# Issuing the first weight transfer of a decode kernel ahead of the entry barrier of the engines

## The chip, the cores and the metric

The kernel runs on one core of a Trainium2 chip. The third batch of runs was on another chip than the first two, so times are compared within a batch. The metric is the device time of one execution in microseconds (us), smaller is better. One execution in each set is also profiled; its span (first to last instruction of the program) is about 1.8 us shorter than the measured time.

Engines are called TensorE (PE in the profile; PEld is its weight load), VectorE (DVE), ScalarE (ACT), GpSimd (POOL) and SyncE (SP). A `q` behind an engine (SPq) marks work of its sequencer, such as issuing a transfer.

## The reference, cut to what matters

One decode step for four sequences: attention over a cache of 8192 keys, and a gated MLP, mixed by a gate.

```python
# B=4, Sq=1, D=1024, H=32, Sk=8192, Dh=128, F=3584; all bfloat16
q = (x @ wq)                                       # wq 1024 x 4096: 8 MB
scores = einsum("bhqd,bhkd->bhqk", q, k_cache) * Dh ** -0.5     # k_cache 256 MB
o = einsum("bhqk,bhkd->bhqd", softmax(scores), v_cache)         # v_cache 256 MB
a = o.reshape(B, 1, H * Dh) @ wo                   # wo 8 MB
b = x + sigmoid(r) * ((silu(x @ w_gate) * (x @ w_up)) @ w_down) # S=1: every row is chosen
return g * a + (1 - g) * b
```

Each key and value is used for one query only, so nearly all of the work is moving 576 MB (549 MiB) from HBM. Sizes called MB in the rest of this text are units of 2^20 bytes, except in lines and rates of the profile.

## The kernel before

All large inputs go through a ring of five slots of 4 MB in SBUF. SyncE issues every ring transfer, in program order; a transfer is issued when the engine that last read its slot has finished with it. K passes through VectorE, which transposes it into a tile T with two buffers, and TensorE multiplies T; V goes straight to TensorE.

```python
ring = const.tile([P, NS, RING], BF, name="ring")          # NS = 5 slots of 4 MB

def load_pair(src, n, apart=False):
    a = slots(2)
    if a + 1 < NS and not apart:                           # one transfer over two slots
        nc.sync.dma_start(out=flat[:, lo:lo + 2 * n], in_=src)
    ...                                                    # else one transfer for each slot

nc.scalar.dma_start(out=x6[0:Bn], in_=x2)                  # and two more tiny loads into x6
...
def k_pair(d):                                             # cut
    ks = load_pair(kv_view(A_k_cache, d), RING)
    for n in range(RD):                                    # 8 pieces
        T = ttp.tile(..., tag="T")                         # bufs=2
        nc.vector.transpose(out=T[...], in_=kn[...])       # frees the slot after piece 4 and 8
        ... 8 matmuls on T ...

def v_pair(d):                                             # cut: the last pair
    vs = [ring[:, slots(1)] for _ in range(2)]
    nc.sync.dma_start(out=vs[0], in_=vv[:, 0:RING])        # 4 MB in one transfer
    for c in range(4):
        nc.sync.dma_start(out=vs[1][:, lo:hi], in_=vv[:, RING + lo:RING + hi])   # 1 MB each
```

The order is: wq, w_gate, then K pairs, w_up, w_down, K and V pairs in turn, and wo at the end. The program begins with a barrier of all engines, made by the framework: each engine drains, GpSimd collects the arrivals and releases all (in the profile of before the drains begin at 0.00 to 0.37 us, GpSimd's two semaphore records stand at 0.59 and 0.67 us, the releases of the others at 0.71 to 0.72 us).

## Time and profile before

| | |
|---|---|
| time, first three runs | 1347.67 us median (1346.08 to 1349.52) |
| span of the profiled run | 1345.3 us |
| TensorE, VectorE busy | 78%, 46% |
| mean granted TensorE clock | 0.91 |
| first packet of the ring | 1.81 us after the program's first instruction |

The page of the kernel before. The second part gives 40 equal slices of the span, with the busy share of the 16 DMA engines in tenths; the third the share of the 16 engines' time that each queue used:

```profile
span 1345.3 us, 7987 instructions
...
DMA  9999999999999999999999999999999999999997
GB/s 413 427 436 427 442 429 425 443 431 419 443 435 419 437 435 433 433 433 430 435 435 435 435 431 431 427 428 434 435 423 442 433 419 431 431 427 440 426 426 318
...
q1 hardware_dynamic: 13976, 575.68, 99.3%
```

The queue is busy from end to end at about 430 GB/s.

The timeline of the kernel before (start, duration, engine, line, operation; in brackets the idle time of the engine before it and what ended it), at the start:

```profile
0.79 0.56 ACTq L122 DMA_DIRECT2D x<-in_A_x_dram  x1
0.80 0.40 SPq L109 DMA_DIRECT2D ring<-in_A_wq_dram  x1
1.25 0.41 SPq L109 DMA_DIRECT2D ring<-in_B_w_gate_dram  x1
...
15.84 0.62 PE L139 MATMUL small<-identb,x 6*128 6x6 bf16 x8 [15.84 <-DMA x<-in_gate_w_dram]
23.21 6.51 PE L226 MATMUL S_ps<-ring,xw 128*4 128x512 bf16 x64 [0.56 <-DMA ring<-in_A_wq_dram]
...
50.85 2.31 DVE L352 STREAM_TRANSPOSE T<-ring 128x2048 uint32<-128x2048 uint32 x1 [17.02 <-DMA ring<-in_A_k_cache_dram]
```

SyncE stands at the barrier from 0.00 to 0.71 us (the trace's records of its drain and release) and issues wq only then. The last line is the first use of K.

The same timeline around the issue of a later K transfer, and at the end of the program:

```profile
1106.94 4.51 DVE L352 STREAM_TRANSPOSE T<-ring 128x2048 uint32<-128x2048 uint32 x2 [3.13 <-DMA ring<-in_A_k_cache_dram]
1109.40 3.57 PE L358 MATMUL S_ps<-T,Z 128*128 128x512 bf16 x8 [7.10 <-DVE T L352]
...
1117.94 4.51 DVE L352 STREAM_TRANSPOSE T<-ring 128x2048 uint32<-128x2048 uint32 x2 [2.48 <-PE S_ps L358]
1120.28 0.33 SPq L109 DMA_DIRECT2D ring<-in_A_k_cache_dram  x1
...
1316.38 13.11 PE L429 MATMUL o_ps<-ring,PB 128*32 128x512 bf16 x60 [1.86 <-DMA ring<-in_A_v_cache_dram]
1335.32 7.07 PE L192 MATMUL acc<-ring,LT 128*4 128x512 bf16 x32 [0.36 <-DVE LT L291]
```

Here the issue at 1120.28 us waits for VectorE, which had waited 2.48 us for TensorE, which ran its eight matmuls in 3.57 us (granted clock 0.5 from 1107.69 us for 10.24 us) where the same group takes 1.90 us elsewhere (at 923.22 us, granted clock 1.0).

### The profile page before, as it was taken

How to read it: one execution, taken by the hardware profiler on the slowest of the kernel's cores; microseconds unless marked ns; L12 is line 12 of the kernel's file. 1: busy time of each engine (PE TensorE's matmuls, PEld its weight loads, DVE VectorE, ACT ScalarE, POOL GpSimd, SP SyncE). 2: the span in 40 equal slices, each digit the busy share in tenths (PEclk: the TensorE clock that was granted, in tenths of full speed). 3: DMA queues.
4: the chain of work that ended last, by engine and by line, in shares of the span. 5: the costliest groups of instructions: out<-in, count | busy, mean ns of one | idle time of the engine just before them, and what ended most of it. 6: DMA issues, size and time to landing. Idle time of an engine off the chain costs nothing.

```text
span 1345.3 us, 7987 instructions
## 1 busy us (share of the span) xinstructions
PE 1050.1 (78%) x4536; PEld 229.2 (17%) x2348; DVE 623.1 (46%) x358; ACT 51.4 (4%) x46; POOL 59.0 (4%) x91
## 2 busy tenths in 40 slices
PE   2565977777887778878977779697779679877888
PEld 0111111112111111111211111111111112111211
DVE  4465655534445553345455456146555254556000
ACT  0000100001000100001000010001000010000000
POOL 4000100001000100001000010000000010000000
PEclk9787988988998888899898889898899798989999
DMA  9999999999999999999999999999999999999997
GB/s 413 427 436 427 442 429 425 443 431 419 443 435 419 437 435 433 433 433 430 435 435 435 435 431 431 427 428 434 435 423 442 433 419 431 431 427 440 426 426 318
DMA packets 14031, 576.20 MB, mean 428 GB/s; under 512 B 1566, under 2 KB 1574, under 8 KB 2092
## 3 DMA queue, kind: packets, MB, share of 16 engines
q1 hardware_dynamic: 13976, 575.68, 99.3%
q8 instruction: 27, 0.44, 0.1%
q14 instruction: 8, 0.07, 0.0%
q10 hardware_dynamic: 20, 0.02, 0.0%
HBM read 575.68 MB, written 0.01 MB: 428 GB/s over the span
## 4 chain that ended last, share of the span: by engine, by line
DMA 58%; PE 23%; DVE 10%; issue 8%; ACT 0%; DVEq 0%; SPq 0%; POOL 0%
DMA ring<-in_A_k_cache_dram 50%; PE S_ps L358 11%; PE o_ps L429 11%; DVE T L352 10%; DMA ring<-in_A_v_cache_dram 5%; DMA ring<-in_B_w_gate_dram 3%; PE small L448 1%; PE acc L192 1%; PE o_ps L226 0%; ACT OS L441 0%; DVEq L352 0%; DVE OS L442 0%; ACT res L495 0%; SPq L109 0%; POOL Z L335 0%
## 5 line engine op out<-in xcount | busy, mean ns | idle before, releaser
L352 DVE STREAM_TRANSPOSE T<-ring 128x2048 uint32<-128x2048 uint32 x256 | 570.6, 2282 | 501.4 <-DMA ring<-in_A_k_cache_dram 425.9
L358 PE MATMUL S_ps<-T,Z 128*128 128x512 bf16 x2048 | 536.7, 410 | 220.8 <-DVE T L352 214.8
L429 PE MATMUL o_ps<-ring,PB 128*32 128x512 bf16 x2048 | 460.5, 387 | 37.6 <-DMA ring<-in_A_v_cache_dram 37.6
L358 PEld LDWEIGHTS <-Z 128*128 128x128 bf16 x1024 | 106.2, 104 | 643.6 <-issue 635.8
L429 PEld LDWEIGHTS <-PB 128*32 128x32 bf16 x1024 | 100.7, 99 | 395.2 <-issue 373.1
L383 ACT ACTIVATE PTs<-S_ps,negm 128x1024 bf16<-128x1024 f32 x8 | 8.9, 1114 | 994.7 <-DVE negm L380 994.7
L335 POOL TENSOR_TENSOR Z<-qa,mq 128x16 bf16<-128x16 bf16 x32 | 8.3, 262 | 808.4 <-PE S_ps L358 737.3
L442 DVE SCALAR_TENSOR_TENSOR OS<-o_ps,mE,OS 128x512 f32<-128x512 f32 x8 | 6.0, 751 | 68.8 <-ACT OS L441 68.8
L394 POOL COPY PB<-PT 32x1024 bf16<-32x1024 bf16 x16 | 30.4, 1897 | 26.8 <-DVE rex L396 26.5
L392 ACT COPY PB<-PT 32x1024 bf16<-32x1024 bf16 x16 | 30.6, 1914 | 10.7 <-DVE PT L385 10.6
L291 DVE CAST LT<-small 128x64 bf16<-128x64 f32 x2 | 0.4, 224 | 46.3 <-PE small L289 46.3
L376 POOL PARTITION_ALL_REDUCE gmx<-mex x8 | 3.2, 396 | 340.6 <-DVE mex L373 340.6
L371 DVE TENSOR_REDUCE m<-S_ps 128x1 f32<-128x1024 f32 x8 | 9.8, 1225 | 15.9 <-PE S_ps L358 15.9
L402 DVE RECIPROCAL rinv<-tot 128x16 f32<-128x16 f32 x8 | 2.0, 248 | 31.1 <-POOL tot L398 31.1
L385 DVE STREAM_TRANSPOSE PT<-PTs 128x1024 bf16<-128x1024 bf16 x8 | 10.0, 1245 | 12.1 <-ACT PTs L383 12.1
L192 PE MATMUL acc<-ring,LT 128*4 128x512 bf16 x64 | 14.5, 379 | 0.7 <-DVE LT L291 0.7
L139 PE MATMUL small<-identb,x 6*128 6x6 bf16 x8 | 0.6, 196 | 15.8 <-DMA x<-in_gate_w_dram 15.8
L448 PEld LDWEIGHTS small<-selg,OS 128*128 128x128 f32 x64 | 11.8, 260 | 7.0 <-issue 4.9
L192 PE MATMUL acc<-ring,hT 128*4 128x512 bf16 x56 | 12.2, 379 | 0.0
L448 PE MATMUL small<-selg,OS 128*128 128x16 f32 x64 | 10.6, 302 | 0.9 <-DVE OS L442 0.9
L226 PE MATMUL o_ps<-ring,xw 128*4 128x512 bf16 x56 | 4.9, 481 | 7.1 <-DMA ring<-in_B_w_gate_dram 7.1
L441 ACT ACTIVATE OS<-o_ps,mE 128x512 f32<-128x512 f32 x8 | 5.5, 687 | 120.2 <-PE o_ps L429 120.2
(71 smaller groups left out, 82.2 us busy)
## 6 DMA issues: line engine op xcount, KB each, us to landing
ring<-in_A_v_cache_dram SPq DMA_DIRECT2D x15, 4096.0 KB, 30.1
ring<-in_A_k_cache_dram SPq DMA_DIRECT2D x14, 4096.0 KB, 31.8
ring<-in_B_w_gate_dram SPq DMA_DIRECT2D x1, 7168.0 KB
ring<-in_B_w_up_dram SPq DMA_DIRECT2D x1, 7168.0 KB
ring<-in_B_w_down_dram SPq DMA_DIRECT2D x2, 3584.0 KB
ring<-in_A_wo_dram SPq DMA_DIRECT2D x6, 1024.0 KB, 27.0
ring<-in_A_v_cache_dram SPq DMA_DIRECT2D x4, 1024.0 KB, 34.0
ring<-in_A_wo_dram SPq DMA_DIRECT2D x4, 512.0 KB, 17.3
```

Source lines behind the costliest of these rows:

```text
L192: nc.tensor.matmul(out_ap, lhsT=lhsT, rhs=rhs, start=start, stop=True, skip_group_check=True)
L335: nc.gpsimd.tensor_tensor(out=Z[:, :, QP - 1:QP - 1 + P].rearrange("p e (q c) -> p e q c", c=QP)[:, :, :, 0], in0=qa[:, :, h0:h0 + NQ, b], ...
L352: nc.vector.transpose(out=T[:].rearrange("p j h i e -> p (j h i e)").bitcast(U32), in_=kn[:, c * CJ * Dh:(c + 1) * CJ * Dh].bitcast(U32))
L358: nc.tensor.matmul(sps[:, z, :], lhsT=Z[:, he, s:s + P], rhs=T[:, 16 * z:16 * z + 16, half, :, e], start=(t == 0 and n == 0 and he == 0), ...
L371: nc.vector.tensor_reduce(out=m1[:], in_=sps[:].rearrange("p z n -> p (z n)"), axis=AX.X, op=ALU.max)
L383: nc.scalar.activation(out=PTs[:], in_=sps[:].rearrange("p z n -> p (z n)"), func=ACT.Exp, bias=negm[:, 0:1], scale=scale, accum_out=rs[:, ...
L385: nc.vector.transpose(out=PT[:].rearrange("p j i -> p (j i)"), in_=PTs[:])
L392: nc.scalar.copy(out=Bv[at, :, :, q, :], in_=Pv[at])
L394: nc.gpsimd.tensor_copy(out=Bv[at, :, :, q, :], in_=Pv[at])
L429: nc.tensor.matmul(o_ps[row:row + NM, e, :], lhsT=B_[:, RD * t + c, z, w].rearrange("p e s j -> p (e s j)"), rhs=vn[:, j0 * Dh:(j0 + 4) * ...
L442: nc.vector.scalar_tensor_tensor(out=o_sb[:], in0=o_ps[:, 1, :], scalar=mE[:, 1:2], in1=o_sb[:], op0=ALU.mult, op1=ALU.add)
L448: nc.tensor.matmul(oT[:, :], lhsT=o_sb[:, q * Dh:(q + 1) * Dh], rhs=selg[:, q].rearrange("p t s -> p (t s)"), start=(q == 0), stop=(q == 3))
```

## The change

The intent: the wq transfer waits for nothing, so its issue is moved in front of SyncE's drain, and the queue starts while the other engines are still at the barrier.

```diff
+def begin_early(nc):
+    for f in nc.m.functions:
+        head = list(f.blocks[0].instructions)
+        ...
+        at = [n for n, i in enumerate(head) if i.engine == SP and isinstance(i, mybir.InstDrain)]
+        for block in f.blocks[1:2]:
+            body = list(block.instructions)
+            n = next(... the first InstDMACopy of SP ...)
+            i = body[n]
+            if at and not (i.sync_info is not None and i.sync_info.on_wait):
+                block.instructions = body[:n] + body[n + 1:]
+                f.blocks[0].instructions = head[:at[0]] + [i] + head[at[0]:]
 ...
     nc.at_finalize(keep_weights)
+    nc.at_finalize(begin_early)
```

(Names of engine types are shortened and blank lines left out.) No other instruction changes its place on any engine.

More of the change, by code (lines that the diff above doesn't have):

```diff
@@ L36, in keep_weights @@
             block.instructions = kept
+def begin_early(nc):
+    for f in nc.m.functions:
+        head = list(f.blocks[0].instructions)
+        if any(isinstance(i, mybir.InstDMACopy) for i in head):
+            continue
+        at = [n for n, i in enumerate(head) if i.engine == mybir.EngineType.SP and isinstance(i, mybir.InstDrain)]
+        for block in f.blocks[1:2]:
+            body = list(block.instructions)
+            n = next(n for n, i in enumerate(body) if i.engine == mybir.EngineType.SP and isinstance(i, mybir.InstDMACopy))
+            i = body[n]
+            if at and not (i.sync_info is not None and i.sync_info.on_wait):
+                block.instructions = body[:n] + body[n + 1:]
+                f.blocks[0].instructions = head[:at[0]] + [i] + head[at[0]:]
 @with_exitstack
```

## The prediction

> **What bounds the kernel.** The DMA queue. The page's DMA row reads 9 tenths in every slice but the last; the queue table gives the SyncE queue 99.3% of the 16 engines' time. Its packet records run from 1.81 us (first wq packet) to 1340.69 us without a pause of the 16 engines together: 575.7 MB in 1338.9 us, 430 GB/s. [...] PE is busy 78%, DVE 46%. Counting bytes issued against bytes moved, at every ring transfer's issue the queue still held at least 2.4 us of earlier work (median 13 us; estimate at 430 GB/s). So the queue never ran dry, and the time is: start of the first packet + 1338.9 us of transfer + a tail of about 4.6 us (last matmuls, conversion, output).
>
> **What the change does.** It moves one DMA issue (wq, 8 MB) in front of SyncE's drain, so that it no longer waits for the entry barrier. Otherwise each engine's list is the same. In the trace SyncE's drain stands at 0.00 us, it is released at 0.71 us, and the wq issue runs 0.795 to 1.198 us; its first packet moves 1.0 us after the issue began.
>
> - Removed: 0.79 us of waiting. New issue at about 0.0 us, first packet at about 1.0 us.
> - Added to the barrier: SyncE arrives 0.40 us (its issue) later. The last arrival today is Pool (drain ends 0.546 us), so the barrier should open at the same time, at worst 0.2 us later. w_gate is issued then, with 19 us of wq ahead of it: no cost.
> - Moved: the three tiny x loads (ScalarE queue) now meet a queue already full of wq packets. Today four of their packets go one per 2.42 us wq packet (7.95 to 15.36 us), and x lands at 15.8 us. [...] One to three more of these packets may now take such a turn: x lands at 15.5 to 21 us (estimate), and the q matmuls may start up to 5 us later than wq lands. They have slack: q is ready at 34 us, the first K half lands at 50.85 us, and the transfer that waits for wq's slot (26.85 us) is issued over 10 us before the queue would be empty.
>
> **On the critical path:** all 0.79 us of the earlier start, nothing of the rest. That is 0.06% of the time. The three runs of before spread over 3.4 us (1346.08 to 1349.52), four times the gain, so the verdict should be "same".
>
> **Predicted:** 1347.67 - 0.8 = 1346.9 us; 8 in 10 between 1345.0 and 1348.9. Faster by over 2%: 0.5%; within 2%: 99%; slower by over 2%: 0.5%.
>
> **What would show it.** In the timeline: wq issue at 0.0 us, first packet at 1.0 us; the landings of wq (23.2), w_gate (40.1) and the first K half (50.85) each about 0.8 us earlier. Barrier release at 0.7 to 0.9 us. x lands the same or later, with no later transfer delayed. DMA share 99% and the tail unchanged.
>
> **What would make it wrong.** The queue's mean rate: 0.1% of it is 1.3 us, more than the gain, so noise may show either sign. The drain may wait for the descriptors and delay everyone. A transfer issued late enough to let the queue run dry would absorb the shift. The measured time may start elsewhere than at SyncE's first instruction.

0.79 us of waiting, taken as 0.8, from 1347.67 us gives 1346.9 us. The 430 GB/s is the rate in the packet records; that it is the most the queue can move was not shown. The estimate for x rests on the starts of its last four packets in the profile of before (7.95, 10.44, 12.86 and 15.36 us) and on the 2.42 us of a 64 KB packet.

## The result and the profile after

| | before | after |
|---|---|---|
| median, us | 1348.13 (1346.08 to 1349.52, 6 runs) | 1348.35 (1345.59 to 1351.52, 6 runs) |
| ratio, 95% interval | | 1.0003 (0.9987 to 1.0018): same |
| span of the profiled run, us | 1345.3 | 1349.7 |

A ratio is the mean time of one kernel's runs over that of the other's runs of the same rounds, so it is not quite the ratio of the medians.

The page after:

```profile
span 1349.7 us, 7987 instructions
...
DMA  9999999999999999999999999999999999999996
GB/s 416 444 432 421 438 426 428 441 435 428 432 430 430 440 435 431 435 431 426 430 434 435 434 430 435 434 419 444 418 422 439 434 425 436 428 423 442 421 424 274
...
q1 hardware_dynamic: 13976, 575.68, 99.1%
```

The timeline after, at the start:

```profile
0.00 0.40 SPq L127 DMA_DIRECT2D ring<-in_A_wq_dram  x1
0.80 0.56 ACTq L140 DMA_DIRECT2D x<-in_A_x_dram  x1
0.81 0.33 SPq L127 DMA_DIRECT2D ring<-in_B_w_gate_dram  x1
...
20.36 0.62 PE L157 MATMUL small<-identb,x 6*128 6x6 bf16 x8 [20.36 <-DMA x<-in_gate_w_dram]
27.19 4.99 PE L244 MATMUL S_ps<-ring,xw 128*4 128x512 bf16 x64
...
49.83 2.31 DVE L370 STREAM_TRANSPOSE T<-ring 128x2048 uint32<-128x2048 uint32 x1 [13.75 <-DMA ring<-in_A_k_cache_dram]
```

The head is as predicted: wq is issued at 0.00 us, its first packet moves at 1.02 us instead of 1.81 us, SyncE is released at 0.72 us (0.71 before), x lands later (20.4 us), and the first K half is there 1.0 us earlier. Yet this profiled run was 4.4 us longer. Its later parts, for the lines shown of before:

```profile
1107.49 4.51 DVE L370 STREAM_TRANSPOSE T<-ring 128x2048 uint32<-128x2048 uint32 x2 [3.06 <-DMA ring<-in_A_k_cache_dram]
1109.95 3.57 PE L376 MATMUL S_ps<-T,Z 128*128 128x512 bf16 x8 [7.03 <-DVE T L370]
...
1118.49 4.50 DVE L370 STREAM_TRANSPOSE T<-ring 128x2048 uint32<-128x2048 uint32 x2 [2.49 <-PE S_ps L376]
1120.83 0.33 SPq L127 DMA_DIRECT2D ring<-in_A_k_cache_dram  x1
...
1317.97 15.89 PE L447 MATMUL o_ps<-ring,PB 128*32 128x512 bf16 x60 [3.54 <-DMA ring<-in_A_v_cache_dram]
1339.70 7.07 PE L210 MATMUL acc<-ring,LT 128*4 128x512 bf16 x32 [0.36 <-DVE LT L309]
```

Two things differ. At 1120.83 us the K issue comes no earlier than before, although the queue had begun earlier. At the end, TensorE waited 3.54 us for the last V pair instead of 1.86 us, and its 60 matmuls then took 15.89 us instead of 13.11 us. The clock records of the trace say why they took longer: in this run the granted clock was 0.5 from 1316.82 us for 6.83 us; in the profiled run of before it was 1.0 from 1305.66 us to 1346.62 us.

### The profile page after: what moved, and what is told of

Same layout as the page of the kernel before. It is cut to its first block, busy times and chain, and to the rows that moved or that the text cites. A ratio compares the mean times of both kernels' runs of the same rounds, so it can differ in the third digit from the quotient of the medians. Undisturbed runs are those within 1.5% of the kernel's fastest.

```text
span 1349.7 us, 7987 instructions
## 1 busy us (share of the span) xinstructions
PE 1049.0 (78%) x4536; PEld 230.2 (17%) x2348; DVE 620.6 (46%) x358; ACT 51.4 (4%) x46; POOL 57.7 (4%) x91
## 4 chain that ended last, share of the span: by engine, by line
DMA 60%; PE 22%; DVE 11%; issue 6%; another core or an unknown queue 0%; ACT 0%; DVEq 0%; SPq 0%
DMA ring<-in_A_k_cache_dram 53%; DVE T L370 11%; PE S_ps L376 10%; PE o_ps L447 10%; DMA ring<-in_A_v_cache_dram 5%; DMA ring<-in_B_w_gate_dram 3%; PE small L466 1%; PE acc L210 1%; PE acc L244 0%; ACT OS L459 0%; DVEq L370 0%; DVE OS L460 0%; ACT res L513 0%; DVE LT L309 0%
## 5 line engine op out<-in xcount | busy, mean ns | idle before, releaser
L410 ACT COPY PB<-PT 32x1024 bf16<-32x1024 bf16 x16 | 30.6, 1913 | 10.7 <-DVE PT L403 10.6
L157 PE MATMUL small<-identb,x 6*128 6x6 bf16 x8 | 0.6, 196 | 20.4 <-DMA x<-in_gate_w_dram 20.4
```

The source lines that it names most:

```text
L410: nc.scalar.copy(out=Bv[at, :, :, q, :], in_=Pv[at])
```

## The experiments

Theory 1: the earlier start reaches the end one for one, and scatter of the runs hides it (the texts also lay the scatter of the end itself to theory 3). Theory 2: the lead is given back because x and the q work come late. Theory 3: the lead is lost on the way, where a ring slot comes free at a time that TensorE's clock sets, while the queue is almost empty. In the expectations of the first batch the last two are not yet told apart, and "theory 2" there means any loss to the ring. Twelve runs were made in three batches; each batch brought its own runs of the kernel before. "±" is 1.96 standard errors of the difference of two means, worked out from the single times.

### Control and repeats

`aa_before` is the kernel before, `after_again` and `after_third` the changed kernel, without an edit.

> The kernel before, unchanged, under a new label: a control. Both theories: ratio 1.000 with the same kernel; single executions spread over about 3 us, as before. If the means of two sets of the same kernel differ by 0.8 us or more, timings of this size cannot show a gain of 0.8 us at all.

> The changed kernel again. Theory 1 (the 0.8 us is gained, and hidden by noise of the end of the program and of the queue's rate): over all runs together the mean is 0.8 us below before, each single profile again has wq issued at 0.0 us, w_gate and the first K half landing 0.3 to 1.0 us earlier, and the end is scattered by several us. Theory 2 (the gain is given back to the ring: a slot is released late, the queue waits): mean equal to before or above it, and the shift of the landings is gone by some 100 us in every profile.

> The changed kernel a third time, to pool. Theory 1 (gain of 0.8 us real, hidden by noise): mean of all its runs below the mean of all runs of before. Theory 3 (the lead is partly lost again where a TensorE half-clock stretch makes a ring slot come free late; the two profiles of the changed kernel show it at 952 to 962 us, and the queue ran partly dry for 0.5 us at 964 us): a profile that has a shorter half-clock stretch there keeps its lead of 0.4 to 1.0 us to the end of the transfers; one that has 10.2 us there loses it.

Ratios: aa_before 1.0000 (0.9988 to 1.0013), after_again 0.9996 (0.9982 to 1.0010), after_third 1.0008 (0.9994 to 1.0022). The control differs by 0.5 us from the other nine runs of the same kernel (1348.14 against 1348.63). The three sets of the changed kernel stand at +0.4, -0.4 and +1.0 us to the before of their own batch, each ±1.7 to 2.0. So sets of this size can't resolve 0.8 us, and something steadier was needed.

The third profile (span 1345.3 us) shows the same place as above in the other of two forms:

```profile
1105.20 4.51 DVE L370 STREAM_TRANSPOSE T<-ring 128x2048 uint32<-128x2048 uint32 x2 [2.05 <-DMA ring<-in_A_k_cache_dram]
1107.66 3.26 PE L376 MATMUL S_ps<-T,Z 128*128 128x512 bf16 x8 [6.01 <-DVE T L370]
...
1113.50 8.89 DVE L370 STREAM_TRANSPOSE T<-ring 128x2048 uint32<-128x2048 uint32 x4
1115.84 0.33 SPq L127 DMA_DIRECT2D ring<-in_A_k_cache_dram  x1
...
1314.62 14.80 PE L447 MATMUL o_ps<-ring,PB 128*32 128x512 bf16 x60 [3.55 <-DMA ring<-in_A_v_cache_dram]
1335.25 7.07 PE L210 MATMUL acc<-ring,LT 128*4 128x512 bf16 x32 [0.35 <-DVE LT L309]
```

With no 2.5 us wait of VectorE for TensorE, the K transfer is issued at 1115.84 us, 5.0 us before the one of the first profile after. The half-clock stretch there was 3.4 us long, against 13.7 us. Not all of the 5.0 us comes from it: VectorE began on the K half 2.3 us earlier (1105.20 against 1107.49 us), and the other 2.7 us lie between that start and the issue (10.6 against 13.3 us).

### The same effect, larger and with the sign turned

```diff
 # both in the kernel before
+    nc.vector.memset(ring[:, 0], 0.0)        # delay_large: also ring[:, 1]
+    for s in (2, 4):
+        nc.vector.memset(ring[:, s, 0:8], 0.0)
     NX = Bn + 2
```

The first three transfers then wait for VectorE.

> The change's effect made larger with the sign turned: in the kernel before, the first three transfers of SyncE wait for a VectorE memset of ring slot 0 (about 7.3 us), so the first packet comes about 7.7 us later. Theory 1 (queue saturated from first packet to end): time +7.7 us (1355.8), slope 1.0 per us of delay of the first packet, within 1.5 us of noise. Theory 2 (ring feedback absorbs shifts): clearly less, under +4 us.

> As the small delay, with two ring slots of memset ahead (about 14.6 us): first packet about 15 us later. Theory 1: +15 us (1363), so that the line through before, the small and the large delay has a slope of 1.0. Theory 2: slope under 0.5.

Timelines of delay_small, then delay_large:

```profile
2.57 6.88 DVE L120 MEMSET ring<- 128x8192 uint32 x1 [2.57 <-issue]
...
9.48 0.39 SPq L109 DMA_DIRECT2D ring<-in_A_wq_dram  x1
```

```profile
11.11 6.88 DVE L121 MEMSET ring<- 128x8192 uint32 x1 [1.66 <-issue]
...
18.02 0.39 SPq L109 DMA_DIRECT2D ring<-in_A_wq_dram  x1
```

The planned 7.3 us was an estimate: eight times the 0.91 us that VectorE's memset of 128x1024 takes in the profile of before; in delay_small the memset of a slot took 6.88 us and began at 2.57 us. The delays came out larger than planned: the first packet is 8.7 and 17.2 us later than before (10.50 and 19.04 us against 1.81 us). Ratios 1.0060 (1.0047 to 1.0073) and 1.0119 (1.0106 to 1.0133); against the 14 runs of the kernel before in this batch that is +7.8 ±1.0 and +15.8 ±1.4 us, about 0.9 us for each us of delay. So a late start is largely paid at the end. A slope under a half is out; a slope of exactly 1 is not needed by these runs, nor does a large delay prove that the last 0.8 us count in full.

### Moving the x loads

```diff
 # x_early, in the changed kernel: the same move for ScalarE's three loads
+            xs = [... first three InstDMACopy of ScalarE ...]
+            f.blocks[0].instructions = head[:at] + xs + head[at:]   # at: ScalarE's drain
 # x_late, in the changed kernel: wq is loaded first, x behind it on the same queue
-    nc.scalar.dma_start(out=x6[0:Bn], in_=x2)
+    nc.sync.dma_start(out=x6[0:Bn], in_=x2)        # and the other two likewise
```

> The changed kernel with the three x loads of ScalarE also ahead of the barrier, so that x lands at about 2 to 8 us instead of 20 us and the q matmuls start as wq lands (22.4 us instead of 27.2). Theory 1: no change of the time against the changed kernel (within 0.8 us); first K half still lands at 49.8 us. Theory 2 (the late x and q work give the gain back): 0.8 us or more faster than the changed kernel, about 1347.3.

> The changed kernel with the x loads made later on purpose: on the SyncE queue behind wq, so x lands at about 22 to 25 us and the q matmuls start at about 29 to 32 us instead of 27.2. Theory 1: no change (the first K half lands at 49.8 us and q is ready by 42 us; w_gate and all else at the same time, within 0.2 us). Theory 2: slower by 1 us or more.

Timelines of x_early, then x_late:

```profile
18.23 0.62 PE L163 MATMUL small<-identb,x 6*128 6x6 bf16 x8 [18.23 <-DMA x<-in_gate_w_dram]
28.14 5.77 PE L250 MATMUL S_ps<-ring,xw 128*4 128x512 bf16 x64
...
49.82 2.31 DVE L376 STREAM_TRANSPOSE T<-ring 128x2048 uint32<-128x2048 uint32 x1 [12.01 <-DMA ring<-in_A_k_cache_dram]
```

```profile
22.92 0.65 PE L158 MATMUL small<-identb,x 6*128 6x6 bf16 x8 [22.92 <-DMA x<-in_A_x_dram]
27.65 6.21 PE L245 MATMUL S_ps<-ring,xw 128*4 128x512 bf16 x64
...
49.66 4.50 DVE L370 STREAM_TRANSPOSE T<-ring 128x2048 uint32<-128x2048 uint32 x2 [11.69 <-DMA ring<-in_A_k_cache_dram]
```

x_early failed as an experiment: issued at 0.12 us, after wq (0.00 us), x still landed at 18.2 us and the q matmuls started no earlier; the barrier also opened 1.0 us later (SyncE was released at 1.68 us). x_late moved x by 2.6 us, but the q matmuls by only 0.5 us. Times: 0.9997 (0.9986 to 1.0009) and 1.0001 (0.9989 to 1.0013). The q matmuls also started at 23.2 us in one profile of the kernel before and 26.3 us in the other (the control), with spans of 1345.3 and 1344.7 us. What counts against theory 2 is that in all eight profiles with the early issue the first K half is used at 49.66 to 49.98 us, with x landing anywhere from 18.2 to 22.9 us, and that the lead is still there at 100 MB (next section). The direct test, x far earlier or later, was not achieved.

### A steadier end, with and without the early issue

```diff
 # tail_quarters: in the changed kernel; tail_only: the same edit in the kernel before
-            nc.sync.dma_start(out=vs[0], in_=vv[:, 0:RING])
-            for c in range(4):
-                nc.sync.dma_start(out=vs[1][:, lo:hi], in_=vv[:, RING + lo:RING + hi])
+            for half in range(2):
+                for c in range(4):
+                    nc.sync.dma_start(out=vs[half][:, lo:hi], in_=vv[:, half * RING + lo:half * RING + hi])
```

> The changed kernel with the first half of the last V pair loaded in four transfers, as the second half already is. In the profiles TensorE waits 1.9 to 3.5 us for that half (4 MB in one transfer), and where it waited 3.5 us its granted clock fell to half and the end took 3.6 us more. Theory 3 (the scatter of the end is this wait and the half clock that follows): the 64 matmuls start up to 7 us earlier, no half-clock stretch in the last 30 us, time 1 to 3 us below the changed kernel and a smaller spread, the end then set by the last wo transfer. If the end is bound by the queue alone: no change.

In the profile of after the granted clock was 0.5 there for 6.83 us, and from the start of the 60 matmuls to the end of the span it took 2.8 us more than before (31.76 against 28.96 us); the 3.6 us of the text is not found in that pair.

> The kernel before (first transfer after the barrier) with only the last V pair's first half in four transfers. This end scatters less (0.6 us against 1.4 to 1.9 us standard deviation in the runs so far), so beside tail_quarters, which differs from it only by the early issue, it measures what the early issue is worth. Theory 1 (the earlier start reaches the end): tail_only is 0.8 us above the tail_quarters kernel, about 1347.8 against 1347.0. Theory 3 (the lead is lost on the way): no difference, within 0.3 us. Alone against before: 0.4 to 1.2 us faster.

> The changed kernel with the quartered half again, to pool with tail_quarters: mean 1347.0, spread under 2 us. Theory 1: 0.8 us below tail_only. Theory 3: equal to tail_only.

> tail_only again, in turn with the other, so that drift of the chip falls on both. Theory 1: 0.8 us above tail_quarters_2 and tail_quarters_3. Theory 3: equal.

> As tail_quarters_2. Theory 1: mean of the three runs of this kernel 0.8 us (0.3 to 1.3) below the mean of both runs of tail_only. Theory 3: under 0.3 us.

The chain of waits of tail_only, then of tail_quarters_2, over the last 30 us:

```profile
1305.99 19.81 DMA ring<-in_A_v_cache_dram
...
1325.86 14.85 DMA ring<-in_A_wo_dram
...
1340.76 1.04 PE acc L192 x4
```

```profile
1305.95 19.80 DMA ring<-in_A_v_cache_dram
...
1325.82 14.82 DMA ring<-in_A_wo_dram
...
1340.68 1.04 PE acc L210 x4
```

Now the last wo transfer sets the end, with four matmuls behind it (1.04 us). TensorE's earlier work is no longer in the chain of these 30 us: in tail_only 28 matmuls at 1301 us took 7.89 us (as in the profile of before, at a granted clock of 0.5 for 3.41 us of them), in tail_only_2 6.20 us, and both spans are 1344.7 us. In the last batch the means are:

| kernel | runs | mean us | standard deviation |
|---|---|---|---|
| before | 9 | 1347.73 | 1.03 |
| tail_only, both sets (issue after the barrier) | 10 | 1346.61 | 0.54 |
| tail_quarters_2 and _3 (issue ahead of it) | 10 | 1346.56 | 1.11 |

Two things follow. First, the early issue brought -0.05 ±0.76 us here, where theory 1 wanted -0.8. This, and the comparisons of early with late issue in the other batches (x_early and x_late counted as early), combined by their precision, give +0.0 ±0.6 us: the full 0.8 us is outside, half of it is not. Second, both tail kernels beat the two kernels of the study: the 20 runs are 1.1 ±0.8 us below before (0.08%). No single ratio excludes 1 (0.9993, 0.9990, 0.9991 and 0.9996 in the last batch and 0.9992 earlier, each with an interval of about ±0.0013), so the gain rests on the pooled runs. Beside the changed kernel of its own batch tail_quarters had a mean of 1346.98 us against 1348.92 us. The spread under 2 us that was expected of the early kernel was missed: it was 2.8 and 3.0 us in tail_quarters_2 and _3.

### Where the lead goes

For each of the 14 profiles, the packet records give the time at which the ring queue had moved a given number of MB, counted by finished packets or, more smoothly, with packets in flight counted by the share of their time that is over. The lead is that time, averaged over the eight profiles with early issue, minus the average over the four with late issue and no delay:

| moved, MB | 31 | 100 | 300 | 395 | 410 | 540 |
|---|---|---|---|---|---|---|
| about, us | 79 | 246 | 732 | 963 | 1000 | 1315 |
| lead by finished packets, us | -0.77 | -0.74 | -0.64 | -0.38 | -0.03 | -0.29 |
| standard error | 0.12 | 0.05 | 0.12 | 0.13 | 0.27 | 0.30 |
| lead by shares, us | -0.71 | -0.72 | -0.62 | -0.40 | -0.20 | -0.29 |
| standard error | 0.03 | 0.04 | 0.11 | 0.10 | 0.15 | 0.30 |

The lead holds for half of the program, then shrinks between 300 and 410 MB, and its scatter grows. Packets end in waves of sixteen, 1 MB together (in the profile of before sixteen between 308.86 and 310.30 us, the next at 311.28 us), so the first count is coarse at a single place, and the sharp loss between 395 and 410 MB is half as large in the second. After 410 MB the mean lead shrinks no further by either count.

K transfers are issued with under 6 us left in the queue at several places (in the profile of before also near 91, 341, 728 and 923 us). Two of them were followed, near 962 and 1120 us. The second in each of the twelve profiles without a delay (backlog: bytes issued less bytes moved, at 430 GB/s; idle: mean idle time of the 16 engines between 1100 and 1150 us, from the number of packets in flight; place: time at which 470 MB were moved, less the mean of the four late profiles):

| profile | half-clock stretch there, us | K issued at, us | backlog, us | idle, us | place at 470 MB, us |
|---|---|---|---|---|---|
| before | 10.2 | 1120.3 | 2.7 | 0.42 | +0.4 |
| aa_before | 10.2 | 1119.2 | 3.9 | 0.41 | 0.0 |
| tail_only | 10.2 | 1119.4 | 3.7 | 0.43 | +0.2 |
| tail_only_2 | 6.8 | 1116.9 | 6.2 | 0.08 | -0.5 |
| after | 13.7 | 1120.8 | 2.5 | 0.30 | +0.9 |
| after_again | 13.7 | 1121.3 | 2.4 | 0.43 | +1.2 |
| x_early | 10.2 | 1120.4 | 2.3 | 0.48 | +0.5 |
| tail_quarters | 10.2 | 1120.5 | 2.4 | 0.40 | +0.6 |
| after_third | 3.4 | 1115.8 | 6.3 | 0.07 | -1.4 |
| x_late | 6.8 | 1116.8 | 5.9 | 0.07 | -1.1 |
| tail_quarters_2 | 6.8 | 1116.8 | 5.6 | 0.07 | -1.5 |
| tail_quarters_3 | 6.8 | 1116.1 | 6.6 | 0.07 | -1.2 |

The profiles fall into two groups without an exception. Where the stretch at half clock lasts 10.2 us or more, VectorE waits for TensorE, the slot comes free at 1119 to 1121 us, in the early profiles no sooner than in the late ones, and the engines run partly dry: the early profiles have no lead there at all (+0.5 to +1.2 against 0.0 to +0.4). Where it lasts 6.8 us or less, the transfer comes 2 to 5 us earlier and the early profiles keep their lead (-1.1 to -1.5 against -0.5, though that is a single late profile). At the first place, near 962 us, the same holds in a weaker form: a stretch of 6.8 us goes with 0.11 to 0.26 us of idle time between 950 and 1000 us, one of 10.2 us with 0.31 to 0.61 us; five of the eight early profiles and one of the four late ones have the longer one.

This grouping was found after the runs. What had been expected in advance, for after_third, was tied to the first place: 10.2 us there loses the lead, less keeps it to the end. That missed. The profiles of after_third, x_late and tail_quarters_3 had 10.2 us there and still led by 0.8 to 1.2 us at 540 MB; x_early and tail_quarters had 6.8 us and led by 0.1 us or not at all.

The records also limit what the second place explains. In all 14 profiles, the delayed ones too, its K transfer is issued 13.3 us after VectorE began on the K half before it where the stretch is long, and 10.6 to 10.8 us after where it is short. So about 2.6 us go with the length of the stretch, and the rest of the 2 to 5 us to the time at which that K half had landed. The early profiles of the two groups stood 0.5 us apart already at 460 MB, just before the place, and the mean lead was the same before and after it (0.25 and 0.31 us at 460 and 470 MB, by shares). The place adds a scatter as large as the lead; it isn't where the mean lead goes.

Which form a profile takes goes with where TensorE's restart falls on the grid of the clock, described below. At the second place TensorE, after over 3 us of idle time, starts again 0.35 to 0.72 us after a grid point in the short form and 0.85 to 2.00 us after one in the long form. At the first place it is 1.04 to 2.28 us in the long form, and at least 2.58 or at most 0.66 us in the short one. No profile of the 14 is an exception at either place. The time at which the K half is there does not decide it alone: VectorE began at 1105.83 us in aa_before (long) and at 1106.23 us in tail_only_2 (short).

In the clock records of the 14 profiles the granted clock is 0.5 or 1.0, the stretches at 0.5 last 3.41, 6.83, 10.24 or 13.65 us (but for the last one, cut off by the end), within a profile they start on one grid of 3.41 us, and the grid lies at another offset to the program in each run (1.77 us in before, 0.97 us in the control of the same kernel). TensorE was not wholly idle before each fall of the clock: over the 14 profiles it was busy for up to half of the grid step before a fall (466 falls, median 14%), for 40% or more of a step after which the clock stayed full, and for 76% or more of the one before a rise; the ends of matmuls in a trace are modelled, so these shares are estimates from it. What makes the clock fall was not shown.

## Why the prediction was right or wrong

- **Number: right.** 1346.9 us was predicted, with 1345.0 to 1348.9; 1348.35 us was measured, "same". The range was wide for the scatter, so the hit says nothing for the sum: a forecast of no gain would have been right as well, and in that sense it was luck.
- **Head of the program: right.** Issue at 0.00 us, first packet at 1.02 us, barrier release 0.01 us later (SyncE's drain, which the text feared might delay everyone, ended at 0.58 us), x at 20.4 us, and no later transfer hurt by x as far as seen. The first packets, wq's, gained 0.79 us; the first K half 1.0 us in the profile. The w_gate landing (39.89 against 40.15 us) gained only 0.3 us in that pair, not the 0.8 us foretold.
- **"So the queue never ran dry": wrong, and with it "all 0.79 us of the earlier start".** This is the step that failed. A backlog of 2.4 us was read as a margin. But one packet of 64 KB takes 2.42 us (median of the 6400 in the profile of before), so 2.4 us of backlog is about one packet for each engine, and the first transfer took 1.0 us from issue to first packet (0.80 to 1.81 us before, 0.00 to 1.02 us after, 9.48 to 10.50 us in delay_small). In the twelve profiles above a backlog of 2.3 to 3.9 us went with 0.30 to 0.48 us of mean idle time, one of 5.6 us or more with 0.07 to 0.08 us. The check for pauses looked at the 16 engines together and could not see that some were idle. In the profile of before the 16 engines idled 0.42 us on average between 1100 and 1150 us, where 0.07 us is usual for 50 us. At that place the next transfer came 10.6 to 10.8 or 13.3 us after VectorE began on a K half, by the form of the half-clock stretch, and the difference of about 2.6 us is three times the lead. In place of the 0.79 us the runs show +0.0 ±0.6 us in the times, and a lead of 0.7 us that is 0.0 to 0.3 us from 410 MB on (standard error up to 0.3 us). That the lead is lost to such waits is argued from these records and not shown: no run changed when a slot comes free and left the start as it was.
- **"The tail unchanged": wrong as a description.** The end hung on TensorE after the last V pair, not on the last packet. In the profiles the wait there was 1.86 us or 3.54 us, and the 60 matmuls took 13.11 us (clock 1.0) or 15.89 us (clock 0.5 for 6.83 us). With that half loaded in quarters too, TensorE's longest wait for a part of the last V pair in the five tail profiles was 0.60 us, and the mean was 1.1 us shorter; the standard deviation fell from 1.03 to 0.54 us without the early issue, but was 1.11 us with it, so the end is not the only source of scatter.
- **"A transfer issued late enough to let the queue run dry would absorb the shift":** the prediction named this risk itself and then gave it no weight in the sum. The runs show that the engines did run partly dry; that this is what takes the lead is the likely reading, not a shown one.
- **Still open:** whether a part of the 0.8 us (up to about half) reaches the end; the runs cannot tell 0 from 0.4 us. Nor is it shown that the early start makes long half-clock stretches more frequent: five of eight against one of four at the first place, and four of eight against three of four at the second, may be chance. That the form goes with the restart's place on the clock's grid, whose offset is another in each run, speaks for chance. The clock itself was not put under control.

## What to carry to other kernels

A queue that looks 99% busy can still have places where the next transfer waits for a compute engine (here 99.3%, and SyncE waited 38 times for VectorE's transposes before an issue, 391.8 us in total); look there at what is left per DMA engine, and compare it with one packet and the issue latency (here 2.4 us left, 2.42 us and 1.0 us), before counting an earlier start as gained. Work out the scatter of the time before trying a change worth 0.06%: here the end's waits on TensorE gave up more (1.1 us, by loading the last large transfer in pieces) than the start had to give. When an effect is too small to time, make it ten times larger with the sign turned, follow the lead through the trace, and remove the noisiest stage in both kernels before comparing.
